# Final projection of a two-model decode kernel: output halves of 208 and 304 columns in place of 256 and 256

## The chip, the cores and the metric

The kernel runs on one core of a Trainium2 chip. The metric is the device time of one execution in microseconds (us), median over several runs. A profiled execution also gives a span: the time from the first to the last instruction that the profiler recorded, about 2 us less than the device time.

Engines are named as in the profile: PE is TensorE (matmuls), PEld its weight loads, DVE is VectorE, ACT is ScalarE, POOL is GpSimd, SP is SyncE, which here only issues transfers. ACTq and SPq are the instruction queues of ScalarE and SyncE, from which transfers are issued. L700 is line 700 of the kernel.

## The reference

Two attention blocks decode one token for a batch of 4, with 32 query heads, 8 key/value heads and a cache of 8192 positions of 128 elements. Block A attends to the whole cache, block B to the last 2048 positions. The two outputs of 512 columns are put side by side.

```python
q = (x @ wq).reshape(B, Sq, Hq, Dh) ...           # x: 4 x 1 x 512
scores = einsum("bhqd,bhkd->bhqk", q, k) * Dh ** -0.5
o = einsum("bhqk,bhkd->bhqd", softmax(scores), v)
out_A = o.reshape(B, Sq, Hq * Dh) @ wo            # 4 x 1 x 512, bfloat16
...
return concatenate([out_A, out_B], axis=-1)       # 4 x 1 x 1024
```

The caches alone are some 168 MB, so nearly all the time goes into loading them and into transposing and multiplying the keys. The change sits in the last piece of `@ wo` for block A.

## The kernel before

The body is a loop over 20 units of work. After it come the last unit's values and the last quarter of the projection of block A, in eight pieces, one for each head. The result is accumulated in two PSUM banks, one for each half of the 512 columns, because two engines then empty them side by side.

```python
H2 = D // 2                                        # D = 512
halves = [SA[(L + 1) % 2][0:Bn, 0:H2], KTB[2][0:Bn, 0:H2]]

def pe_seed(pe):                                   # puts the sum so far (fp32) into both banks: L679
    ins = None
    for hf in range(2):
        ins = pe.matmul(out=halves[hf], lhsT=identf[0:Bn, 0:Bn], rhs=oacc[:, hf * H2:(hf + 1) * H2], start=True, stop=False)
    return ins
# ... [cut: the last unit's values, in three loads]
for i, n in enumerate(WCH):                        # eight loads of the weight, one head each
    for hq in range(h0, h0 + n):
        for hf in (1, 0):                          # half 1 (ScalarE's) first
            # lfn: the matmul of L700; waits for piece i of the weight, ("WL", i)
            pe.matmul(out=halves[hf], lhsT=OT_sb[:, 0, NSEG - 1, hq, :], rhs=Wl_sb[:, hq, hf * H2:(hf + 1) * H2],
                      start=False, stop=(hq == C - 1))
# ... [cut: bookkeeping]
op("dve", lambda dve: dve.tensor_copy(out=osb[:, 0, 0:H2], in_=halves[0]), waits=[("fin", 0)], inc=("ocp", NTURN))        # L704
op("act", lambda act: act.activation(out=osb[:, 0, H2:D], in_=halves[1], func=ACTF.Copy), waits=[("fin", 1)], inc=("Ef",))  # L705
op("act", dma(out[:, 0, H2:D], osb[:, 0, H2:D]), waits=[("Ef",)], inc=("out", 2))
# ... [cut: SyncE's loads]
op("sp", dma(out[:, 0, 0:H2], osb[:, 0, 0:H2]), waits=[("ocp", NTURN)], inc=("out", 0))
# SyncE then waits for out 1, 2 and 0, and the program ends
```

## Time and profile before

| what | before |
|---|---|
| time, first three runs | 439.19 us (438.82 to 439.37) |
| span of the profiled run | 437.0 us |
| busy share of PE / DVE / ACT / DMA queue of SyncE | 84 / 48 / 45 / 99% |
| copy of half 0, VectorE, 256 columns | 412 ns |
| copy of half 1, ScalarE, 256 columns | 373 ns |
| start of the last pair of matmuls | 434.47 us |

The share of 99% is from the page's list of transfer queues: the kernel is fed at 423 GB/s nearly all the time. The timeline of the end and the waits of SyncE are in the prediction below. Here is the same end cut into stretches. The columns are the stretch, its length, then for each engine its busy time and in brackets its instructions, then the granted clock, the share of time in which the transfer engines were busy, and GB/s.

```profile
432.40:432.76 0.36, 0.08 (x3) 0.00 (x0) 0.18 (x1) 0.00 (x0) 0.00 (x0) 1.00 0.94 305
432.76:434.87 2.11, 2.06 (x16) 1.12 (x16) 0.00 (x0) 0.09 (x1) 0.00 (x0) 1.00 0.33 110
434.87:435.33 0.46, 0.00 (x0) 0.00 (x0) 0.41 (x1) 0.28 (x1) 0.00 (x0) 1.00 0.00 0
435.33:436.56 1.23, 0.00 (x0) 0.00 (x0) 0.00 (x0) 0.00 (x0) 0.00 (x0) 1.00 0.01 3
436.56:437.04 0.48, 0.00 (x0) 0.00 (x0) 0.00 (x0) 0.00 (x0) 0.00 (x0) 1.00 0.00 0
```

Read it from the bottom: 0.48 us of closing barrier, then 1.23 us in which no engine works and almost no bytes move (the output, 4 KB in all, on its way), then 0.46 us of copies, then the projection. The largest piece after the last matmul is a wait for a transfer that moves next to nothing. The share of 1% in it says that its cost is latency, not bandwidth.

### The profile page before, as it was taken

What the parts mean: (1) busy time and instruction counts of PE and PEld (TensorE: products, weight loads), DVE (VectorE), ACT (ScalarE), POOL (GpSimd) and SP (SyncE); (2) the same over time, 40 slices, a digit from 0 to 9 for tenths busy, and PEclk for the clock granted to TensorE, in tenths of its full rate; (3) what the DMA queues carried; (4) which work ended last, traced back from release to release, by engine and by line L of the source; (5) the groups of instructions that cost most, each with busy time, mean ns of one, the idle gap of its engine ahead of it and who ended that gap; (6) DMA issues with size and microseconds to landing.
All of it is one profiled execution on the core that took longest, in us unless ns stands there. A gap on an engine that the chain in (4) does not pass through costs nothing.

```text
span 437.0 us, 15525 instructions
## 1 busy us (share of the span) xinstructions
PE 365.0 (84%) x7174; PEld 337.9 (77%) x7184; DVE 210.0 (48%) x406; ACT 195.0 (45%) x249; POOL 27.7 (6%) x88
## 2 busy tenths in 40 slices
PE   0168898998998959895989598969868996989996
PEld 0158897997997949795979588868868886979975
DVE  0004455664564634563456247525643563455651
ACT  1024473573653625371634254434534462536530
POOL 6100000000000000000000000000100000000000
PEclk9999999999999988999999899989996999799999
DMA  8999999999999999999999999999999999999996
GB/s 340 430 421 421 429 412 430 418 439 412 445 432 432 424 438 432 432 432 432 432 432 429 432 432 430 431 433 432 410 454 432 432 432 432 432 432 411 447 407 255
DMA packets 10996, 184.73 MB, mean 423 GB/s; under 512 B 1236, under 2 KB 2280, under 8 KB 2408
## 3 DMA queue, kind: packets, MB, share of 16 engines
q1 hardware_dynamic: 10960, 184.56, 99.1%
q8 instruction: 8, 0.13, 0.1%
q14 instruction: 4, 0.03, 0.0%
q10 hardware_dynamic: 24, 0.01, 0.0%
HBM read 184.56 MB, written 0.01 MB: 422 GB/s over the span
## 4 chain that ended last, share of the span: by engine, by line
PE 54%; DMA 40%; issue 2%; DVE 1%; SPq 1%; ACT 1%
DMA K_sb<-in_A_k_cache_dram 29%; PE KT L283 27%; PE OT L338 11%; DMA K_sb<-in_B_k_cache_dram 7%; PE SB L322 5%; PE SA L322 4%; DMA V_sb<-in_A_v_cache_dram 4%; PE KT L396 4%; PE SA L350 1%; PE KT L338 1%; SPq L566 1%; DVE oacc L404 1%; PE KT L263 1%; ACT KT_sb L299 1%; DVE OS L501 0%
## 5 line engine op out<-in xcount | busy, mean ns | idle before, releaser
L283 PE MATMUL KT<-identf,K_sb 128*128 128x128 f32 x1280 | 207.6, 296 | 44.1 <-DMA K_sb<-in_A_k_cache_dram 30.7
L299 ACT ACTIVATE KT_sb<-KT 128x1024 bf16<-128x1024 bf16 (+1 forms) x192 | 165.1, 881 | 120.6 <-PE KT L283 120.6
L283 PEld LDWEIGHTS KT<-identf,K_sb 128*128 128x128 f32 x1280 | 147.6, 150 | 49.3 <-DMA K_sb<-in_A_k_cache_dram 31.7
L299 DVE COPY KT_sb<-KT 128x512 int32<-128x512 int32 x160 | 110.5, 691 | 132.1 <-PE KT L283 130.7
L338 PE MATMUL OT<-PT,V_sb 128*128 128x64 bf16 x2560 | 78.1, 193 | 1.6 <-issue 1.1
L338 PEld LDWEIGHTS OT<-PT,V_sb 128*128 128x128 bf16 x2560 | 75.9, 98 | 1.8 <-issue 1.2
L469 ACT ACTIVATE PT<-Dt 128x512 bf16<-128x512 f32 x40 | 24.6, 630 | 84.0 <-DVE Dt L458 84.0
L322 PEld LDWEIGHTS SA<-RQc,KT_sb 128*128 128x128 bf16 x1280 | 56.9, 98 | 2.3
L322 PEld LDWEIGHTS SB<-RQc,KT_sb 128*128 128x128 bf16 x1280 | 51.1, 97 | 7.9 <-issue 4.4
L322 PE MATMUL SA<-RQc,KT_sb 128*128 128x16 bf16 x1280 | 56.4, 170 | 0.0
L322 PE MATMUL SB<-RQc,KT_sb 128*128 128x16 bf16 x1280 | 52.9, 170 | 0.0
L420 DVE TENSOR_REDUCE M<-SB 128x8 f32<-128x512 f32 (+1 forms) x20 | 13.8, 692 | 50.0 <-PE SB L322 50.0
L441 POOL PARTITION_ALL_REDUCE MB<-M1m x20 | 7.7, 387 | 334.3 <-DVE M1m L434 334.3
L396 PE MATMUL KT<-Wo_sb,OL 128*4 128x512 bf16 x80 | 18.9, 379 | 0.0
L201 PE MATMUL KT<-ident,x_sb 4*128 4x4 bf16 x8 | 0.6, 170 | 19.9 <-POOL identf L537 19.9
L201 PEld LDWEIGHTS KT<-ident,x_sb 4*128 4x128 bf16 x8 | 0.4, 112 | 20.1 <-issue 20.1
L476 DVE TENSOR_REDUCE LB<-SA 128x8 f32<-128x512 f32 (+1 forms) x20 | 13.7, 684 | 2.8 <-PE SA L350 2.8
L458 DVE TENSOR_TENSOR Dt<-SA,MBm 128x512 f32<-128x512 f32 x20 | 13.8, 692 | 0.7
L367 DVE TENSOR_TENSOR ORx<-KT,MSK 32x1024 bf16<-32x1024 bf16 x10 | 12.1, 1211 | 3.3 <-PE KT L362 3.3
L458 DVE TENSOR_TENSOR Dt<-SB,MBm 128x512 f32<-128x512 f32 x20 | 13.6, 681 | 0.0
L420 DVE TENSOR_REDUCE M<-SA 128x8 f32<-128x512 f32 (+1 forms) x20 | 13.6, 681 | 0.0
L350 PE MATMUL SA<-PT,onesb 128*128 128x128 bf16 x168 | 12.7, 218 | 0.0
(69 smaller groups left out, 118.0 us busy)
## 6 DMA issues: line engine op xcount, KB each, us to landing
K_sb<-in_A_k_cache_dram SPq DMA_DIRECT2D x15, 4096.0 KB, 22.5
V_sb<-in_A_v_cache_dram SPq DMA_DIRECT2D x15, 4096.0 KB, 30.3
K_sb<-in_B_k_cache_dram SPq DMA_DIRECT2D x8, 2048.0 KB, 23.6
V_sb<-in_B_v_cache_dram SPq DMA_DIRECT2D x16, 1024.0 KB, 18.4
V_sb<-in_B_wq_dram SPq DMA_DIRECT2D x1, 4096.0 KB, 12.5
V_sb<-in_A_wq_dram SPq DMA_DIRECT2D x1, 4096.0 KB, 21.8
Wo_sb<-in_B_wo_dram SPq DMA_DIRECT2D x4, 1024.0 KB, 11.9
K_sb<-in_A_k_cache_dram SPq DMA_DIRECT2D x2, 2048.0 KB, 17.5
```

Of the source, the lines that this page charges most:

```text
L283: ins = pe.transpose(out=bkf[:, pi * 128:(pi + 1) * 128], in_=K_sbf[:, slot, t0:t0 + 2, :].rearrange("p t d -> p (t d)"), identity=identf[ ...
L299: ins = e.tensor_copy(out=d, in_=r) if eng == "dve" else e.activation(out=d, in_=r, func=ACTF.Copy)
L322: ins = pe.matmul(out=stb[:, t % NTH * C:(t % NTH + 2) * C], lhsT=ktv[:, pi, :, e], rhs=RQc[:, u % 2, t // TS, e, :], start=(e == 0), stop ...
L338: ins = pe.matmul(out=otb[:, s * NW:s * NW + w], lhsT=V_sb[:, slot, t, :], rhs=PT[:, slot, t * C:t * C + w], start=(j == 0), stop=(j == n ...
L350: ins = pe.matmul(out=SA[u % 2][:, s * NM:(s + 1) * NM], lhsT=onesb[:, :], rhs=PT[:, u % 2, c0:c0 + NM], start=(i == 0), stop=(i == n - 1))
L367: return dve.tensor_tensor(out=ORx[:, :, :, :], in0=bk[0:NR, 0:128].rearrange("p (i o r) -> p r o i", o=1, r=C).broadcast_to([NR, C, C, 12 ...
L396: ins = pe.matmul(out=bk[0:Bn, 0:D], lhsT=OL[:, i, :], rhs=Wo_sb[:, i, :], start=(i == 0), stop=(i == C - 1))
L420: return dve.tensor_reduce(out=M1[:, h * n:(h + 1) * n].rearrange("p (s h) -> p s h", h=C), in_=bank[:, :].rearrange("p (s j h) -> p s h j ...
L441: return pool.partition_all_reduce(MB[:, 0:n], M1m[:, 0:n], channels=128, reduce_op=ReduceOp.max)
L458: return dve.tensor_tensor(out=Dt[:, h * NTH * C:(h + 1) * NTH * C].rearrange("p (s j h) -> p s j h", s=Sh, h=C), in0=bank[:, :].rearrange ...
L469: return act.activation(out=PT[:, u % 2, a:b], in_=Dt[:, a:b], func=ACTF.Exp, scale=scale)
L476: return dve.tensor_reduce(out=LB[:, 0:n].rearrange("p (s h) -> p s h", h=C), in_=SA[u % 2][:, 0:NSEG * NM].rearrange("p (s j h) -> p s h ...
```

## The change

VectorE's half is the one that ends last before the change. The change moves 48 of its 256 columns to ScalarE, which starts 0.11 us earlier and needs less time per column, so that both copies end together.

```diff
-        H2 = D // 2
-        halves = [SA[(L + 1) % 2][0:Bn, 0:H2], KTB[2][0:Bn, 0:H2]]
+        CUT = [0, 208, D]
+        halves = [SA[(L + 1) % 2][0:Bn, 0:CUT[1]], KTB[2][0:Bn, 0:D - CUT[1]]]
 ... (seed matmuls: CUT[hf]:CUT[hf + 1] for hf * H2:(hf + 1) * H2)
 ... (L700: the same)
-        op("dve", lambda dve: dve.tensor_copy(out=osb[:, 0, 0:H2], in_=halves[0]), ...)
-        op("act", lambda act: act.activation(out=osb[:, 0, H2:D], in_=halves[1], func=ACTF.Copy), ...)
-        op("act", dma(out[:, 0, H2:D], osb[:, 0, H2:D]), ...)
+        op("dve", lambda dve: dve.tensor_copy(out=osb[:, 0, 0:CUT[1]], in_=halves[0]), ...)
+        op("act", lambda act: act.activation(out=osb[:, 0, CUT[1]:D], in_=halves[1], func=ACTF.Copy), ...)
+        op("act", dma(out[:, 0, CUT[1]:D], osb[:, 0, CUT[1]:D]), ...)
 ...
-        op("sp", dma(out[:, 0, 0:H2], osb[:, 0, 0:H2]), ...)
+        op("sp", dma(out[:, 0, 0:CUT[1]], osb[:, 0, 0:CUT[1]]), ...)
```

More of the change, by code (lines that the diff above doesn't have):

```diff
@@ L678, in pe_seed @@
             for hf in range(2):
-                ins = pe.matmul(out=halves[hf], lhsT=identf[0:Bn, 0:Bn], rhs=oacc[:, hf * H2:(hf + 1) * H2], start=True, stop=False)
+                ins = pe.matmul(out=halves[hf], lhsT=identf[0:Bn, 0:Bn], rhs=oacc[:, CUT[hf]:CUT[hf + 1]], start=True, stop=False)
             return ins
@@ L699, in lfn @@
                     def lfn(pe, hq=hq, hf=hf):
-                        return pe.matmul(out=halves[hf], lhsT=OT_sb[:, 0, NSEG - 1, hq, :], rhs=Wl_sb[:, hq, hf * H2:(hf + 1) * H2],
+                        return pe.matmul(out=halves[hf], lhsT=OT_sb[:, 0, NSEG - 1, hq, :], rhs=Wl_sb[:, hq, CUT[hf]:CUT[hf + 1]],
                                          start=False, stop=(hq == C - 1))
@@ L703, in bass_concat_heads__gqa_block_cached__sliding_block_cached__decode_kernel @@
             h0 += n
-        op("dve", lambda dve: dve.tensor_copy(out=osb[:, 0, 0:H2], in_=halves[0]), waits=[("fin", 0)], inc=("ocp", NTURN))
-        op("act", lambda act: act.activation(out=osb[:, 0, H2:D], in_=halves[1], func=ACTF.Copy), waits=[("fin", 1)], inc=("Ef",))
-        op("act", dma(out[:, 0, H2:D], osb[:, 0, H2:D]), waits=[("Ef",)], inc=("out", 2))
+        op("dve", lambda dve: dve.tensor_copy(out=osb[:, 0, 0:CUT[1]], in_=halves[0]), waits=[("fin", 0)], inc=("ocp", NTURN))
+        op("act", lambda act: act.activation(out=osb[:, 0, CUT[1]:D], in_=halves[1], func=ACTF.Copy), waits=[("fin", 1)], inc=("Ef",))
+        op("act", dma(out[:, 0, CUT[1]:D], osb[:, 0, CUT[1]:D]), waits=[("Ef",)], inc=("out", 2))
         def kv_load(kind, u):
@@ L768, in bass_concat_heads__gqa_block_cached__sliding_block_cached__decode_kernel @@
             h0 += n
-        op("sp", dma(out[:, 0, 0:H2], osb[:, 0, 0:H2]), waits=[("ocp", NTURN)], inc=("out", 0))
+        op("sp", dma(out[:, 0, 0:CUT[1]], osb[:, 0, 0:CUT[1]]), waits=[("ocp", NTURN)], inc=("out", 0))
         def full(key):
```

## The prediction

> **What bounds the kernel now.** I read the page first, for the body of the kernel, then the chain of waits and the timeline of the last 3 us, because the whole diff sits in code that runs once, after the loop. On the page, part 1 says which engine is busiest and part 4 names the chain of work that ended last:
>
> ```profile
> PE 365.0 (84%) x7174; PEld 337.9 (77%) x7184; DVE 210.0 (48%) x406; ACT 195.0 (45%) x249; POOL 27.7 (6%) x88
> PE 54%; DMA 40%; issue 2%; DVE 1%; SPq 1%; ACT 1%
> DMA K_sb<-in_A_k_cache_dram 29%; PE KT L283 27%; PE OT L338 11%; DMA K_sb<-in_B_k_cache_dram 7%; PE SB L322 5%; PE SA L322 4%; DMA V_sb<-in_A_v_cache_dram 4%; PE KT L396 4%; PE SA L350 1%; PE KT L338 1%; SPq L566 1%; DVE oacc L404 1%; PE KT L263 1%; ACT KT_sb L299 1%; DVE OS L501 0%
> ```
>
> The reader is to see that TensorE and the loads of the caches carry 94% of a span of 437.0 us, and that neither of the lines that the diff touches (the projection matmuls of L700, the copies of L704 and L705) is large enough to be listed. The chain is what counts, not the busy shares: VectorE's 48% and ScalarE's 45% say nothing about an end that is a few short steps in a row.
>
> The groups of instructions, shapes kept apart, size the lines that change:
>
> ```profile
> L700 PE MATMUL SA<-Wl_sb,OT_sb 128*4 128x256 bf16 x8 | 1.9, 272 | 0.0
> L700 PE MATMUL KT<-Wl_sb,OT_sb 128*4 128x256 bf16 x8 | 1.9, 272 | 0.3 <-issue 0.3
> L679 PE MATMUL SA<-oacc,identf 4*4 4x256 f32 x2 | 0.6, 374 | 0.0
> L679 PE MATMUL KT<-oacc,identf 4*4 4x256 f32 x2 | 0.6, 374 | 0.0
> L704 DVE CAST osb<-SA 4x256 bf16<-4x256 f32 x1 | 0.4, 412 | 2.2 <-PE SA L700 2.2
> L705 ACT ACTIVATE osb<-KT 4x256 bf16<-4x256 f32 x1 | 0.4, 373 | 9.4 <-PE KT L700 9.4
> ```
>
> The last two are the copies out of PSUM: one instruction each, 412 ns on VectorE and 373 ns on ScalarE. The timeline of the end puts them in order (columns: start in us, length in us, engine, line, operation):
>
> ```profile
> 434.47 0.08 PEld L700 LDWEIGHTS KT<-Wl_sb,OT_sb 128*4 128x4 bf16 x1 [0.23 <-DMA Wl_sb<-in_A_wo_dram]
> 434.47 0.27 PE L700 MATMUL KT<-Wl_sb,OT_sb 128*4 128x256 bf16 x1
> 434.48 0.08 PEld L700 LDWEIGHTS SA<-Wl_sb,OT_sb 128*4 128x4 bf16 x1
> 434.58 0.27 PE L700 MATMUL SA<-Wl_sb,OT_sb 128*4 128x256 bf16 x1
> 434.78 0.37 ACT L705 ACTIVATE osb<-KT 4x256 bf16<-4x256 f32 x1 [9.44 <-PE KT L700]
> 434.89 0.41 DVE L704 CAST osb<-SA 4x256 bf16<-4x256 f32 x1 [2.20 <-PE SA L700]
> 435.18 0.27 ACTq L566 DMA_DIRECT2D out_dram<-osb  x1
> 435.33 0.29 SPq L566 DMA_DIRECT2D out_dram<-osb  x1
> ```
>
> Three things are to be seen. The last pair of matmuls starts when the last eighth of the weight has landed, at 434.47, so TensorE's own work before it is not what sets the end. ScalarE's half is finished first: its matmul starts 0.11 us ahead of VectorE's, its copy begins 0.11 us earlier (434.78 against 434.89) and its store is issued 0.15 us earlier (435.18 against 435.33). And the VectorE half is the one that ends last. The waits of SyncE's queue confirm the last step (columns: who waits, for whom, total, times, longest):
>
> ```profile
> SPq L566 <- DVE osb L704: 7.4, 1, 7.4
> SPq L820 <- DMA out_dram<-osb: 0.9, 1, 0.9
> ```
>
> After it has issued its store, SyncE waits 0.9 us for the output's landing and the program ends. In the trace's landing records the store of ScalarE lands at 436.36 and that of SyncE at 436.55, so each needs about 1.2 us from issue (436.36 - 435.18 = 1.18; 436.55 - 435.33 = 1.22), and SyncE's is last by 0.18 us. The program's closing barrier fills the rest, to 437.0. So what the diff can win or lose lies between 434.47 and 436.55, and the part of it that depends on the split is two copies of 0.4 us.
>
> **What the Trainium skill says.** "VectorE: DVE Perf Modes", section "The TRN2 errata": a copy from PSUM to SBUF costs 120 + columns cycles of 0.96 GHz on VectorE and 172 + columns cycles of 1.2 GHz on ScalarE. For 256 columns that is 392 and 357 ns; the trace has 412 and 373, so the page is 4 to 5% low and its order is right. What I take from it are the slopes, 1.04 and 0.83 ns a column. The trace agrees for ScalarE: the 128x1024 and 128x512 activations of the key copies average 1024 and 595 ns, which is 0.84 ns a column. "TensorE: Matmul & The Clock Gate", section "Back-to-back issue gap": 262 cycles of 2.4 GHz, 109 ns, for 256 columns; the trace has starts 0.11 us apart (434.47 to 434.58). "DMA: Bandwidth & Descriptors", section "Anatomy of one DMA", calls most of a transfer's fixed cost the write receipt and not the bytes; the two stores of 2 KB fit that, at 1.2 us each with packets that take 25 to 28 ns. The same page's "Specifications" says that below 512 bytes the engine reads, modifies and writes. The output rows are exactly 512 bytes now; no run so far shows a smaller one.
>
> **The change part by part.** The projection's 512 output columns were cut 256 + 256 and are now 208 (VectorE, SyncE) + 304 (ScalarE). No instruction is added or removed, no wait changes, and the banks in PSUM are the same.
>
> Matmuls. Each of the eight pairs, and the pair of seeds, has 512 columns before and after, so a pair takes the same time. Only the border within it moves. ScalarE's half goes first, and at 109 ns for 256 columns it takes 304/256 x 109 = 129 ns: the ScalarE half of the last pair is done 20 ns later, the VectorE half at the same time. The seeds (L679) lie ahead of the wait for the last piece of V and are the same 512 columns too.
>
> VectorE's path. The copy has 48 columns fewer: 48 x 1.04 = 50 ns less, 412 becomes 362 ns. It starts at 434.89 as before and ends at 435.25; the store goes out at 435.28 and, with the same 1.22 us, lands at 436.50.
>
> ScalarE's path. The copy starts 20 ns later, at 434.80, and has 48 columns more: 48 x 0.84 = 40 ns, 373 becomes 413 ns. Its store goes out at 435.18 + 0.06 = 435.24 and lands at 436.42.
>
> The sum. The later of the two landings moves from 436.55 to 436.50: 0.05 us of 437 us, 0.01%. ScalarE still arrives 0.08 us ahead, so the lead of 0.18 us is used up in the right direction and not overdone. The gain is smaller than the spread of the three runs of before, 439.37 - 438.82 = 0.55 us. With it the time would be 439.19 - 0.05 = 439.14 us.
>
> **The rivals.** First, the stores get in each other's way. They were issued 0.15 us apart and will be 0.04 us apart; if they share DMA engines, they may queue. For it speaks that each packet group in the trace occupies 0.1 us (ScalarE's four rows start between 435.94 and 436.00, SyncE's between 436.09 and 436.15), so they would now overlap. Against it: the packets are under 30 ns, and there is nothing else on the queues then. Cost if it holds: at most the 0.1 us of one group, which turns -0.05 into +0.05 us.
>
> Second, the rows of VectorE's half shrink to 208 x 2 = 416 bytes, under the 512 of the page. A read before the write could add part of a round trip. The trace has no number for that; if it cost a quarter of the 1.22 us landing time, the end would move +0.3 us, which is 0.07%. That is my main reason for giving the upper side some room.
>
> Third, ScalarE becomes the bound. It would need 0.08 us more than my sum on its path (a slower copy, or a store of 608-byte rows cut into two packets). In that case the gain is gone, and the time is 439.2.
>
> Fourth, the split is hidden anyway, because something other than the stores sets the end. The wait of 0.9 us on the output at the end speaks against it; if it held, the time is 439.19.
>
> All four end within 0.3 us of where the kernel stands, and none can reach 2%, which would be 8.8 us: that is four times the 2.1 us between the start of the last matmul pair and the last landing. Only a slow state of the chip or a hidden change of the body could do that, and the loop's code is not touched.
>
> **Range and chances.** I predict 439.15 us: the sum, with a little taken back for the first two rivals. The 8-in-10 range is set by the spread between runs (0.55 us over three), by the rivals (-0.05 to +0.3), and by the other run's own median: 438.6 to 439.8. Faster by over 2% and slower by over 2% get half a per cent each.
>
> **What would show it.** In the changed kernel's profile the VectorE copy should last about 362 ns and the ScalarE copy about 413; the ScalarE copy should begin about 0.09 us ahead of VectorE's and not 0.11; the two stores should be issued within 0.06 us; matmul pairs should stay 0.21 us apart. A landing later than 1.25 us after its issue would speak for the collision or for the short rows, according to whether both stores or only SyncE's is late. The wait of SyncE on the output should be about 0.9 us still. The prediction is wrong if the span moves by more than 1 us with the last 3 us unchanged in shape: then something in the body has moved that I do not see in the diff.

## The result, and the profile after

| | before | after |
|---|---|---|
| time, median of 6 runs each | 439.11 us (438.82 to 439.42) | 439.05 us (438.98 to 439.76) |
| ratio after / before | | 1.0002, 95% interval 0.9989 to 1.0015 |
| span of the profiled run | 437.0 us | 437.2 us |
| start of the last matmul pair (call it T) | 434.473 us | 434.517 us |
| last landing of the output, after T | 2.073 us | 2.153 us |

A ratio here is the mean time of one kernel's runs over the mean of the other's of the same rounds, so it is not quite the ratio of the medians. What the change does is far under what the time can show, so the rest is read from the traces, and always from T on. T itself, the end of the kernel's body, moved between 434.31 and 434.74 us in the twelve traces, and no kernel here touches the body. That 0.43 us of scatter is more than anything the end of the kernel can give, and a bare span must not be read as the effect of a split.

The timeline of the end of the changed kernel (start in us, length, engine, line, operation):

```profile
434.52 0.08 PEld L700 LDWEIGHTS KT<-Wl_sb,OT_sb 128*4 128x4 bf16 x1 [0.22 <-DMA Wl_sb<-in_A_wo_dram]
434.52 0.29 PE L700 MATMUL KT<-Wl_sb,OT_sb 128*4 128x304 bf16 x1
434.52 0.08 PEld L700 LDWEIGHTS SA<-Wl_sb,OT_sb 128*4 128x4 bf16 x1
434.65 0.25 PE L700 MATMUL SA<-Wl_sb,OT_sb 128*4 128x208 bf16 x1
434.85 0.41 ACT L705 ACTIVATE osb<-KT 4x304 bf16<-4x304 f32 x1 [10.13 <-PE KT L700]
434.94 0.36 DVE L704 CAST osb<-SA 4x208 bf16<-4x208 f32 x1 [2.18 <-PE SA L700]
435.29 0.27 ACTq L566 DMA_DIRECT2D out_dram<-osb  x1
435.32 0.29 SPq L566 DMA_DIRECT2D out_dram<-osb  x1
```

The groups of the changed kernel give the sizes (busy us, mean ns of one):

```profile
L700 PE MATMUL KT<-Wl_sb,OT_sb 128*4 128x304 bf16 x8 | 1.9, 291 | 0.3 <-issue 0.3
L700 PE MATMUL SA<-Wl_sb,OT_sb 128*4 128x208 bf16 x8 | 1.8, 252 | 0.0
L705 ACT ACTIVATE osb<-KT 4x304 bf16<-4x304 f32 x1 | 0.4, 413 | 10.1 <-PE KT L700 10.1
L704 DVE CAST osb<-SA 4x208 bf16<-4x208 f32 x1 | 0.4, 363 | 2.2 <-PE SA L700 2.2
```

The copies did what they should: they now end within 0.04 us of each other, and SyncE's store goes out 0.81 us after T, where it went out at 0.86 before (435.33 - 434.47). The waits of SyncE in the changed kernel (who waits, for whom, total, times, longest):

```profile
SPq L566 <- DVE osb L704: 7.4, 1, 7.4
SPq L820 <- DMA out_dram<-osb: 1.1, 1, 1.1
```

The last wait of the program has grown from 0.9 to 1.1 us. That is where the 0.05 us went, and more. The trace's landing and packet records give the same in nanoseconds. A store leaves eight packets, its four rows and a packet of 4 bytes after each; its landing is the last of the increments of its semaphore:

| us | before, ScalarE | before, SyncE | after, ScalarE | after, SyncE |
|---|---|---|---|---|
| issued, after T | 0.711 | 0.858 | 0.771 | 0.808 |
| first packet starts, after T | 1.467 | 1.613 | 1.536 | 1.635 |
| landed, after T | 1.889 | 2.073 | 1.969 | 2.153 |
| issue to landing | 1.178 | 1.215 | 1.198 | 1.345 |

SyncE's store was issued 0.050 us earlier and landed 0.080 us later. The last landing plus 0.50 us of barrier is the end of the span in both traces. So the span's 0.12 us are 0.04 us of T and 0.08 us of slower landing.

### The profile page after: what moved, and what is told of

It reads as the page before. It is cut to its first block, busy times and chain, and to the rows that moved or that the text cites. A ratio compares the mean times of both kernels' runs of the same rounds, so it can differ in the third digit from the quotient of the medians.

```text
span 437.2 us, 15535 instructions
## 1 busy us (share of the span) xinstructions
PE 365.5 (84%) x7184; PEld 337.5 (77%) x7184; DVE 209.8 (48%) x406; ACT 194.9 (45%) x249; POOL 27.6 (6%) x88
## 4 chain that ended last, share of the span: by engine, by line
PE 50%; DMA 41%; PEld 4%; issue 2%; DVE 1%; SPq 1%; ACT 1%; PEldq 0%
DMA K_sb<-in_A_k_cache_dram 29%; PE KT L283 24%; PE OT L338 10%; DMA K_sb<-in_B_k_cache_dram 7%; DMA V_sb<-in_A_v_cache_dram 4%; PE SB L322 4%; PE SA L322 4%; PE KT L396 3%; PEld KT L283 2%; PE SA L350 1%; PE KT L338 1%; PE KT L263 1%; PEld OT L338 1%; SPq L566 1%; PEld SA L322 1%
```

## The experiments

There were three theories of why SyncE's store became slower, and a fourth came out of the first batch:

- **Q**: its packets queue behind ScalarE's, which were issued 0.04 us earlier.
- **R**: its rows of 416 bytes are slow because they are under 512.
- **N**: it is scatter from run to run.
- **F**: the second store can't land sooner than 0.185 us after the first, whatever its rows and its packets do.

All experiments but one are single profiled looks (their state can't be told from one run, so none of their times is compared); what is compared is measured from T within each trace. The table has them all; each is told below it. "First" and "second" are in order of issue.

| kernel | first store | first issued | second issued | first landed | second landed | between landings |
|---|---|---|---|---|---|---|
| before | ScalarE, 512 B rows | 0.711 | 0.858 | 1.889 | 2.073 | 0.184 |
| before, again | ScalarE, 512 | 0.712 | 0.858 | 1.887 | 2.071 | 0.184 |
| after | ScalarE, 608 | 0.771 | 0.808 | 1.969 | 2.153 | 0.184 |
| after, again | ScalarE, 608 | 0.771 | 0.808 | 1.963 | 2.148 | 0.185 |
| mirror | ScalarE, 416 | 0.652 | 0.908 | 1.833 | 2.100 | 0.267 |
| actlate | SyncE, 416 | 0.808 | 0.835 | 1.981 | 2.169 | 0.188 |
| order256 | SyncE, 512 | 0.748 | 0.820 | 1.917 | 2.105 | 0.188 |
| c240 | ScalarE, 544 | 0.731 | 0.841 | 1.914 | 2.097 | 0.183 |
| c16 | SyncE, 32 | 0.634 | 1.011 | 1.764 | 2.262 | 0.498 |
| c272 | ScalarE, 480 | 0.690 | 0.874 | 1.865 | 2.055 | 0.190 |
| first216 | SyncE, 432 | 0.690 | 0.854 | 1.862 | 2.049 | 0.187 |
| onestore | SyncE, 1024 | 0.866 | none | 2.118 | none | none |

### The changed kernel again

No edit.

> The changed kernel once more, for the scatter. In its first trace the SyncE store took 1.34 us from issue to landing (the kernel before: 1.22) and the ScalarE store 1.20 (1.18). Theory Q (the SyncE store queues behind the ScalarE store, issued 0.04 us earlier) and theory R (rows of 416 bytes are confirmed later than rows of 512): again 1.32 to 1.36 us for SyncE and 1.18 to 1.21 for ScalarE. Theory N (scatter from run to run): SyncE anywhere between 1.2 and 1.36.

Measured: 1.340 us for SyncE and 1.192 for ScalarE, against 1.345 and 1.198 in the first trace. N falls: two traces agree to 0.006 us, although their T differ by 0.13 us.

### The split turned round

```diff
-        CUT = [0, 208, D]
+        CUT = [0, 304, D]
```

> The split turned round, 304 columns for VectorE and 208 for ScalarE: copies 412 + 48 x 1.04 = 462 ns and 373 - 48 x 0.83 = 333 ns, stores issued about 0.26 us apart, ScalarE first, so they can't queue; the short rows are now ScalarE's. Q: ScalarE 1.18 us and SyncE 1.22, no cost anywhere. R: ScalarE 1.24 (0.06 more), SyncE 1.22. In both the last landing is about 2.13 us after the start of the last matmul pair, 0.05 us more than in the kernel before (2.08).

The timeline of this kernel's end:

```profile
434.94 0.33 ACT L705 ACTIVATE osb<-KT 4x208 bf16<-4x208 f32 x1 [9.62 <-PE KT L700]
435.07 0.46 DVE L704 CAST osb<-SA 4x304 bf16<-4x304 f32 x1 [2.18 <-PE SA L700]
435.31 0.27 ACTq L566 DMA_DIRECT2D out_dram<-osb  x1
435.56 0.29 SPq L566 DMA_DIRECT2D out_dram<-osb  x1
```

The stores go out 0.256 us apart. ScalarE's, now the one with rows of 416 bytes, took 1.181 us, no more than with 512; R would have had 1.24. SyncE's took 1.192, which is less than the 1.215 of the kernel before. That was not expected and is the first sign that even there it had been held up a little. The last landing, 2.100, is 0.05 us ahead of the changed kernel's, although VectorE's copy is 0.1 us longer.

### ScalarE's store moved behind SyncE's

A copy of 16 columns into an unused tile `dly` (its declaration is cut here) stands between ScalarE's copy and its store, which waits for it.

```diff
+        op("act", lambda act: act.activation(out=dly[0:Bn, 0:16], in_=halves[1][:, 0:16], func=ACTF.Copy), inc=("Ef", 1))
-        op("act", dma(out[:, 0, CUT[1]:D], osb[:, 0, CUT[1]:D]), waits=[("Ef",)], inc=("out", 2))
+        op("act", dma(out[:, 0, CUT[1]:D], osb[:, 0, CUT[1]:D]), waits=[("Ef", 1)], inc=("out", 2))
```

> The changed kernel with a small extra ScalarE copy ahead of the ScalarE store, which is so issued some 0.15 us after the SyncE store and not ahead of it; SyncE's rows are still 416 bytes. Q: SyncE back at 1.22 us from issue to landing, ScalarE at 1.18. R: SyncE stays above, 1.28 if the 0.07 us after the last packet is the rows' and the other 0.07 us the queue's, 1.34 if all is the rows'.

The timeline of this kernel's end (its lines are shifted by one or two):

```profile
435.06 0.41 ACT L706 ACTIVATE osb<-KT 4x304 bf16<-4x304 f32 x1 [10.16 <-PE KT L701]
435.15 0.36 DVE L705 CAST osb<-SA 4x208 bf16<-4x208 f32 x1 [2.15 <-PE SA L701]
435.38 0.16 ACT L707 ACTIVATE dly<-KT 4x16 bf16<-4x16 f32 x1
435.54 0.29 SPq L567 DMA_DIRECT2D out_dram<-osb  x1
435.57 0.27 ACTq L567 DMA_DIRECT2D out_dram<-osb  x1
```

The delay came out at 0.03 us behind SyncE and not the 0.15 expected, because the extra copy began before the first had ended. It serves all the same: SyncE's store is first. With the same 416 bytes a row and the same issue time of 0.808 it took 1.173 us, where it takes 1.345 when it is second. R falls. ScalarE's store, now second and with rows of 608 bytes, took 1.334 us against 1.198. The slow store is the second one, whichever engine issues it and however long its rows are.

### Rows of 512 bytes, the order of the matmuls turned round

```diff
-                for hf in (1, 0):
+                for hf in (0, 1):
```

in the kernel before.

> The kernel before (256 + 256, rows of 512 bytes) with VectorE's matmul first in each pair: VectorE's copy starts 0.11 us earlier, ScalarE's 0.11 later, and the stores go out within 0.08 us, SyncE first. Q: the second store, ScalarE's, starts its packets when SyncE's end and takes 1.20 to 1.25 us, SyncE 1.22. R: no cost, SyncE 1.22 and ScalarE 1.18, and the last landing is 0.05 us nearer to the last pair's start than before, 2.03 for 2.08 us.

The timeline of this kernel's end, and SyncE's last wait, which is for both stores:

```profile
434.76 0.41 DVE L704 CAST osb<-SA 4x256 bf16<-4x256 f32 x1 [2.05 <-PE SA L700]
434.87 0.37 ACT L705 ACTIVATE osb<-KT 4x256 bf16<-4x256 f32 x1 [10.22 <-PE KT L700]
435.20 0.29 SPq L566 DMA_DIRECT2D out_dram<-osb  x1
435.27 0.27 ACTq L566 DMA_DIRECT2D out_dram<-osb  x1
```

```profile
SPq L820 <- DMA out_dram<-osb: 1.1, 1, 1.1
```

Both stores are out by 0.820, earlier than the later one of the kernel before (0.858). Yet the last landing is at 2.105, which is 0.03 us later. ScalarE's store took 1.285 us with rows of full 512 bytes, more than Q had allowed: its first packet came 0.791 us after its issue, 0.026 to 0.035 more than for the first store of the traces above (0.756 to 0.765), and the rest of the delay of about 0.1 us came after the packets. The two landings are 0.188 us apart. Laid beside the others, the last column of the table came out: in the five traces so far where the stores go out within 0.15 us, the landings lie 0.184 to 0.188 us apart. That is F, and it contradicts the prediction's fixed latency: in these traces the second landing follows the first landing, not its own issue.

### The kernel before again, and a split in between

The repeat has no edit; the split is

```diff
-        CUT = [0, 208, D]
+        CUT = [0, 240, D]
```

> The kernel before once more. The first batch suggests theory F: the second store lands at the earliest 0.185 us after the first, whatever its rows (0.184 to 0.188 in five traces), so the SyncE store of the kernel before was already held by the ScalarE store. F: ScalarE 1.18 us, SyncE 1.21 us, landings 0.184 us apart, last landing 2.07 us after the start of the last matmul pair. Theory R (short rows cost) fell with the run that delays ScalarE's store and isn't expected to show here.

> 240 columns for VectorE, 272 for ScalarE, so rows of 480 bytes; ScalarE's store is issued 0.73 us after the last pair's start and lands at 1.91, SyncE's is issued at 0.84. F: SyncE lands 0.185 us after ScalarE, at 2.09 to 2.10. Free stores of 1.19 us (no floor): 2.03. The prediction's rule, SyncE's issue plus 1.22: 2.06.

The repeat gave 1.175 and 1.213 us, landings 0.184 apart and 2.071 after T. The 240-column split gave this end:

```profile
435.01 0.39 ACT L705 ACTIVATE osb<-KT 4x272 bf16<-4x272 f32 x1 [9.85 <-PE KT L700]
435.11 0.40 DVE L704 CAST osb<-SA 4x240 bf16<-4x240 f32 x1 [2.17 <-PE SA L700]
435.43 0.27 ACTq L566 DMA_DIRECT2D out_dram<-osb  x1
435.54 0.29 SPq L566 DMA_DIRECT2D out_dram<-osb  x1
```

SyncE landed at 2.097, 0.183 us after ScalarE: F had said 2.09 to 2.10, the prediction's rule 2.06, free stores 2.03. Going from 256 to 240 columns, SyncE's store is issued 0.017 us earlier and lands 0.024 us later, because ScalarE's, the first one, is issued 0.020 us later. In this trace no packet queues: SyncE's first packet starts 0.758 us after its issue (1.599 - 0.841), as in the kernel before (0.755), and 0.014 us after ScalarE's last row has ended. The time is lost after the packets, until the landing: 0.408 us from the end of SyncE's last packet, where ScalarE's store takes 0.324. So Q, as a queue of packets, is not what holds the second store either; in the changed kernel it adds 0.07 us to the start of the packets (1.635 - 0.808 = 0.827), but the landing would be held all the same.

### Very short rows, far ahead of the other store

```diff
-        CUT = [0, 208, D]
+        CUT = [0, 16, D]
```

> 16 columns for VectorE and 496 for ScalarE, so SyncE's rows have 32 bytes and its store goes out some 0.4 us ahead of ScalarE's. F: nothing holds either, SyncE 1.17 to 1.19 us, ScalarE (second now) 1.18 to 1.20, copies of 163 and 573 ns, last landing near 2.20 us after the last pair's start. R in any form (a fixed extra for rows under 512 bytes): SyncE 1.25 us or more.

SyncE's rows of 32 bytes took 1.130 us, less than any other store here, so nothing is left of R. VectorE's copy took 163 ns and ScalarE's 573, as expected. ScalarE's store, second by 0.377 us and so not held, took 1.251 us, above the 1.18 to 1.20 expected, and the last landing, 2.262, is 0.06 us later than expected. Its rows of 992 bytes took 45 to 47 ns a packet where those of 512 take 25 to 28, so rows that long have a cost of their own, which I had not counted.

### One store for both halves

```diff
-        op("act", dma(out[:, 0, CUT[1]:D], osb[:, 0, CUT[1]:D]), waits=[("Ef",)], inc=("out", 2))
... [cut: SyncE's loads]
-        op("sp", dma(out[:, 0, 0:CUT[1]], osb[:, 0, 0:CUT[1]]), waits=[("ocp", NTURN)], inc=("out", 0))
+        op("sp", dma(out[:, 0, 0:D], osb[:, 0, 0:D]), waits=[("Ef",), ("ocp", NTURN)], inc=("out", 0))
... [cut]
-            for i in (1, 2, 0):
+            for i in (1, 0):               # SyncE's last waits
```

> The copies of the changed kernel (208 and 304 columns), but one store of 1024-byte rows by SyncE after both. Its issue waits for VectorE's copy alone (ends 0.78 us after the last pair's start, ScalarE's 0.74), so it goes out at 0.81. F: with no other store ahead it takes 1.17 to 1.20 us and lands at 1.98 to 2.02, 0.13 to 0.17 us nearer than in the changed kernel (2.15) and 0.05 to 0.09 nearer than before (2.07). If the larger transfer itself is slower: 2.1 or more. Over the whole time this is 0.02%, within 2% either way.

This is a miss for F's figure; the landing is in the range given for a larger transfer that is slower by itself. The timeline of its end:

```profile
435.07 0.36 DVE L704 CAST osb<-SA 4x208 bf16<-4x208 f32 x1 [2.16 <-PE SA L700]
435.52 0.29 SPq L566 DMA_DIRECT2D out_dram<-osb  x1
```

The store goes out 0.866 us after T, 0.058 us later than expected: SyncE now has two waits ahead of it, and between the end of VectorE's copy and the issue lie 0.084 us where there were 0.027 in the changed kernel. It then needs 1.252 us, with rows of 1024 bytes and packets of 45 to 48 ns. It lands at 2.118: ahead of the changed kernel by 0.035 us, behind the kernel before by 0.045. Five timed runs against nine of the kernel before gave 439.08 us (438.73 to 439.68) and 439.26, ratio 0.9996, interval 0.9983 to 1.001: the same. It speaks neither for nor against F.

### Two splits that F would choose

F, with a free latency of 1.19 us, gives a rule for the last landing: the later of (first landing + 0.185) and (second issue + 1.19). It says how far apart the stores should be issued: about 0.17 us (0.185 + a first latency of 1.175 - 1.19). More columns for VectorE than 256 give that in the present order; with VectorE first, fewer do.

```diff
-        CUT = [0, 208, D]
+        CUT = [0, 272, D]          # c272
```
```diff
-        CUT = [0, 208, D]
+        CUT = [0, 216, D]          # first216
-                for hf in (1, 0):
+                for hf in (0, 1):
```

> 272 columns for VectorE, 240 for ScalarE: the other side of the kernel before. ScalarE's store goes out at 0.69 us after the last pair's start and lands at 1.87; SyncE's goes out at 0.875. F (the last landing is the later of the first landing + 0.185 and the second issue + 1.19): 2.06 to 2.07, the two limits meet, 0.01 under the kernel before. The prediction's rule (SyncE's issue + 1.22): 2.095.

> The split that F would choose: VectorE's matmul first in each pair and 216 columns for VectorE, 296 for ScalarE. SyncE's store goes out first, at 0.69, and lands at 1.865; ScalarE's at 0.855. F: last landing 2.04 to 2.06 us after the last pair's start, 0.02 to 0.03 nearer than in the kernel before (2.07) and 0.10 nearer than in the changed one (2.15). If F is wrong and a store simply takes 1.22 us: 2.07 to 2.08.

The timeline of the second one's end:

```profile
434.67 0.37 DVE L704 CAST osb<-SA 4x216 bf16<-4x216 f32 x1 [2.06 <-PE SA L700]
434.80 0.41 ACT L705 ACTIVATE osb<-KT 4x296 bf16<-4x296 f32 x1 [9.93 <-PE KT L700]
435.07 0.29 SPq L566 DMA_DIRECT2D out_dram<-osb  x1
435.23 0.27 ACTq L566 DMA_DIRECT2D out_dram<-osb  x1
```

They landed at 2.055 and 2.049 us after T, 0.018 and 0.024 us ahead of the kernel before, and 0.098 and 0.104 ahead of the changed one. The 272-column kernel came out 0.005 us under the range of F and 0.040 under the prediction's rule; the other lies in F's range. The two copies of `first216` end 0.16 us apart (434.67 + 0.37 = 435.04 and 434.80 + 0.41 = 435.21, less the rounding), further apart than those of the changed kernel (0.04 us), and its output lands earlier. Its 0.02 us can't be seen in a time of 439 us with a spread of half a microsecond. The two are the best ends found here, as read from one trace each, not kernels shown to be faster.

The packet records bear F out. From the end of its last packet to its landing, every store that is first, alone, or issued at least 0.16 us after the other takes 0.321 to 0.330 us (0.304 with rows of 32 bytes). The seven second stores issued within 0.15 us take 0.364 to 0.434. So the second stores of `c272` and `first216` (0.324 and 0.327) were no longer held, although they too land 0.19 us after the first: F's two limits meet there.

## Why the prediction was right, and which step of it failed

The time was right: 439.15 predicted, 439.05 measured, inside the range of 438.6 to 439.8. It was right mainly by its bound: the 2.1 us from the last pair of matmuls to the last landing were all that the split could act on. That 439.05 lies so close to 439.15 says nothing for the sum, whose 0.05 us drown in a spread of half a microsecond, and whose sign the trace contradicts.

- *Matmuls.* The ScalarE half of the last pair was to be done 20 ns later and VectorE's at the same time. ScalarE's copy starts 0.329 us after T against 0.308, VectorE's 0.418 against 0.417. Right.
- *Copies.* 362 and 413 ns were predicted; 363 and 413 were measured. Right, and the slopes of 1.04 and 0.83 ns a column hold down to 16 columns on VectorE (163 ns) and up to 496 on ScalarE (573).
- *Issue of the stores.* They were to be 0.04 us apart, SyncE's 0.05 us earlier. Measured 0.037 and 0.050. Right.
- *Landing of SyncE's store.* This is the step that failed: "with the same 1.22 us, lands at 436.50". The 1.22 us were taken as a property of the store. The runs show that they were not, even in the kernel before: that store would have needed about 1.19 us by itself (1.192 in `mirror`), and was held until 0.184 us after ScalarE's landing. Issuing it earlier could therefore gain nothing, and since ScalarE's store was issued 0.060 us later, the end went back by 0.080 us. The sum's "-0.05" was in truth +0.08.
- *"ScalarE still arrives 0.08 us ahead, so the lead ... is used up in the right direction".* The lead was not slack. In no trace do the two landings come closer than 0.183 us, and the kernel before, at 0.184, already stood there.
- *First rival, the stores get in each other's way.* Right in kind. Its cost was given as at most 0.1 us, from the overlap of the packets; SyncE's store lost 0.130 us (1.345 - 1.215), about half of it after its packets.
- *Second rival, rows under 512 bytes.* Wrong: 1.173 us with 416 bytes and 1.130 with 32, when no other store is ahead. The prediction's own sign pointed here: a landing later than 1.25 us, of SyncE's store alone, was to speak for the short rows. Only SyncE's was late (1.345 against 1.198), yet the rows were not the cause; a store that follows another closely is late alone, too.
- *Third rival, ScalarE becomes the bound.* In the changed kernel its own landing was not last, but its issue time sets the end through the distance between the landings. *Fourth rival, the split is hidden:* the stores do set the end.

What makes the distance of about 0.185 us stays open. The Trainium skill, "DMA: Bandwidth & Descriptors", section "Queues, rings and completion order", says that a semaphore increment lands only after every earlier write from that transfer engine, across its queues. That would fit two stores whose rows are on the same engines: the increments of both then come in a fixed order. No run here shows on which engines the rows lie, or whether the writes to memory themselves are what takes 0.185 us (both stores write into the same four rows of the output). The landing records narrow it a little: in the seven traces where the second store is held, each of its four increments comes 0.177 to 0.188 us after the increment of the same number of the first store, while the increments of one store are 0.010 to 0.041 us apart. So it is not that any two landings need 0.18 us. An experiment with the two stores on different engines would tell; with four rows each I saw no way to choose the engines.

## What to carry to other kernels

When two small stores end a kernel, do not take it that they should leave together: here the second landed no sooner than 0.183 us after the first, so that with issues within 0.15 us the first landing set the end and not the second issue, and the best splits issued them about 0.16 to 0.18 us apart. A latency read for one transfer from a trace can already contain a wait for another; compare it with the same transfer alone before using it in a sum. And when the piece that a change acts on is 2 us of 439, bound the effect first and read it from a mark inside the trace, as the body alone scattered by 0.43 us.

## What the Trainium skill lacked or had wrong

- "DMA: Bandwidth & Descriptors" has no figure for the least distance between the landings of two small stores issued close together: 0.183 to 0.188 us here in seven traces with issues 0.03 to 0.15 us apart. With issues 0.16 us apart or more, the second store was not held, and the landings were 0.187 us apart or more.
- No page says how long a store issued from SyncE or ScalarE takes to land after its last packet: 0.321 to 0.330 us here where no other store held it (0.304 with rows of 32 bytes). Most of the 1.18 us or so passed earlier, 0.752 to 0.765 us of it between issue and first packet.
- "DMA: Bandwidth & Descriptors", section "Specifications", has a read-modify-write below 512 bytes. If it happens, these stores do not show it: 416-byte rows took 1.173 and 1.181 us and 32-byte rows 1.130 us from issue to landing, against 1.17 to 1.18 us for 512-byte rows. What took longer were rows of 992 and 1024 bytes (1.25 us).
- "VectorE: DVE Perf Modes", section "The TRN2 errata", is low by a fixed amount for these copies of 4 partitions out of PSUM: 412, 363 and 163 ns for 256, 208 and 16 columns are 140 cycles + columns at 0.96 GHz, not 120; and 373, 413 and 573 ns for 256, 304 and 496 columns on ScalarE are 192 cycles + columns at 1.2 GHz, not 172. The slopes are right.
